# One scaled product per chunk instead of seven levels of pairwise decays, with the old way kept in a conditional block

## The chip, the cores and the metric

The kernel runs on one core of one Trainium2 chip. The metric is device time in microseconds from one launch. Before the change the median of three runs is 1061.55 us (1060.96 to 1065.03).

## The reference, cut to what matters

A linear recurrence with a decay per head and channel, and then a dense layer. B, H, S, D are 4, 8, 768, 48; there are 3072 tokens of width 384, and the dense layer is 2048 wide. The decays `w` are drawn between 0.85 and 0.95; the weights of the dense layer come as float64.

```
for t in range(S):
    cur = einsum('bhd,bhe->bhde', u[None] * kt, vt)
    y[:, :, t] = einsum('bhd,bhde->bhe', rt, state + cur)
    state = w[None, :, :, None] * state + einsum('bhd,bhe->bhde', kt, vt)
x = y.transpose(0, 2, 1, 3).reshape(B * S, H * D)
h = x @ w_in
out = (h - tanh(h)) @ w_out
```

## The kernel before

**First part.** Time is cut into 6 chunks of 128 steps. A unit (`unit`, L186) is one chunk of one batch, all 8 heads; there are 24 units, in order of chunk, then batch. Two heads share the 128 partitions (64 each, of which 48 are used), so a unit has four pairs of heads. Within a chunk, step t reads step s < t with the weight w^(t-1-s). The kernel never forms a negative power: it takes blocks of 128, 64, ... 2 steps, and pairs the steps of a block's first half with those of its second. For each of the six larger sizes POOL multiplies the turned r with powers (`rl`, L218), DVE the turned k (`kl`, L221); TensorE then makes the product of each of the seven levels (`lev`, L246, four pairs of heads, each product two instructions), and a copy puts it into the table `at`: ScalarE for the first level (L248), DVE under a mask for the other six (L250). `lev` has two buffers. Then `y_p` (L261, L265) applies `at` to v and, from the second chunk, the scaled r (`rs`, L232) to the state; `kv_p` (L273) makes the state's increment from `kn` (L228); three transposes (L289) lay the tokens out for the second part. The turned k and r come from transposes (L199) through one buffer and ScalarE copies (L201, L204). The step's own product through `u` is made on POOL (`rk`, L207 and L208) and DVE.

**Second part.** `dense` (L294) takes a block of two units' tokens; there are 12 blocks. For each of eight pairs of columns of `w_in` it makes `h` (L301), then on ScalarE, POOL and DVE h - tanh(h) with a series where h is small (L312 to L321), and two pairs later the product with `w_out` (L327). The output goes out by two DMAs per block (L343).

**Weights.** 28 pieces of float64 are loaded through two staging buffers by DMAs on ScalarE's queue (L147) and turned into float32 by one ScalarE, five DVE and two POOL instructions each (L154 to L161).

**Order.** `weave` (L357) interleaves the steps of several streams in proportion: the units of blocks 0 and 1 with the weights, then each dense block j with the units of block j + 2. Within that, a planner that works with estimated times sets the order of each engine's instructions. Every engine then runs its own list in order. At the start POOL clears thirty buffers (L119) that keep zeros, and DVE grows tables of powers by doubling (L88 to L94).

Of the kernel before, what the change touches and what calls it, by code (L numbers as in the profile page):

```python
# [25 lines left out]
@with_exitstack  # L26
def kernel(
    ctx: ExitStack,
    tc: tile.TileContext,
    r: bass.AP,  # L30
    k: bass.AP,
    v: bass.AP,
    w: bass.AP,
    u: bass.AP,
    moe_w_in: bass.AP,
    moe_w_out: bass.AP,
    out: bass.AP,
):
    nc = tc.nc
    V, A, T, G = nc.vector, nc.scalar, nc.tensor, nc.gpsimd  # L40

    B, H, S, D = r.shape
    DM, DFF = moe_w_in.shape
    C = 128                  # steps of time in a chunk
    PAD = 64                 # partitions of a head where two of them share the 128
    NP = H // 2              # pairs of heads
    NCH = S // C
    NU = NCH * B             # units of work: a chunk of one batch, all heads
    NK = DM // 128
    NF = DFF // 128  # L50
    L = 2                    # units in a block of the dense part
    NT = L * C
    SIZES = [128, 64, 32, 16, 8, 4, 2]
    AHEAD = 2
    HEAD = [slice(i * PAD, i * PAD + D) for i in range(2)]   # partitions of a pair's heads

    const = ctx.enter_context(tc.tile_pool(name="const", bufs=1))
    load = ctx.enter_context(tc.tile_pool(name="load", bufs=3))
    stage = ctx.enter_context(tc.tile_pool(name="stage", bufs=2))
    work = ctx.enter_context(tc.tile_pool(name="work", bufs=2))  # L60
    gpool = ctx.enter_context(tc.tile_pool(name="gpool", bufs=6))
    ps_a = ctx.enter_context(tc.tile_pool(name="ps_a", bufs=1, space=PSUM))
    ps_d = ctx.enter_context(tc.tile_pool(name="ps_d", bufs=2, space=PSUM))

    def fixed(name, shape, dt=F32):
        return const.tile(shape, dt, name=name, tag=name)

    ident = fixed("ident", [128, 128])
    make_identity(nc, ident)

# [4 lines left out]
    with nc.allow_non_contiguous_dma(reason="384 numbers, once"):  # L75
        for i in range(2):
            nc.sync.dma_start(out=wcol[i * PAD : i * PAD + D, :], in_=w.rearrange("(p i) d -> i d p", i=2)[i])
    ub = fixed("ub", [128, H, D])
    nc.sync.dma_start(
        out=ub.rearrange("p h d -> p (h d)"),  # L80
        in_=bass.AP(tensor=u.tensor, offset=u.offset, ap=[[0, 128], [1, H * D]]),
    )
# [50 lines left out]
    w_in_sb = fixed("w_in_sb", [128, NK, DFF])  # L133
    w_out_sb = fixed("w_out_sb", [128, NF, DM])
# [3 lines left out]
    def weight(dst, src, cols):  # L138
        if src.dtype == F32:
            return lambda: nc.scalar.dma_start(out=dst, in_=src)  # L140
        # Bits of float64 to float32, rounded to the nearest: the upper word gives sign, exponent
        # and 20 bits; the lower word, scaled to the exponent, is added.
# [23 lines left out]
    for q in range(DFF // 512):  # L166
        for ko in range(NK):
            sl = slice(q * 512, (q + 1) * 512)
            weights.append(weight(w_in_sb[:, ko, sl], w_in_v[:, ko, sl], 512))
        for f in range(4 * q, 4 * q + 4):  # L170
            weights.append(weight(w_out_sb[:, f, :], w_out_v[:, f, :], DM))

# [13 lines left out]
    def unit(n, xt, slot):  # L186
        """Steps of unit n; the last writes its tokens, transposed, to xt[:, :, slot, :]."""
        c, b = divmod(n, B)
        if n + AHEAD < NU:
            fetch(n + AHEAD)  # L190
# [4 lines left out]
        rT = rTs[n % 2]      # rT[:, p, i]: head 2 p + i, zero on the other head's partitions  # L195
# [9 lines left out]
        # The step's own key and value, through u.  # L205
# [86 lines left out]

# [1 line left out]
    def dense(j, xt):  # L294
        outs = [ps_d.tile([128, DM], F32, name=f"o{i}", tag=f"o{i}", bufs=1) for i in range(L)]

        def first(f):
            h = ps_d.tile([128, 2, NT], F32, name="h", tag="h")
            for z in range(2):
                for kk in range(NK):  # L300
                    T.matmul(h[:, z], w_in_sb[:, kk, (f + z) * 128 : (f + z + 1) * 128],  # L301
                             xt[:, kk].rearrange("p b t -> p (b t)"),
                             start=kk == 0, stop=kk == NK - 1)
            hf = h.rearrange("p z t -> p (z t)")

            def tmp(name):
                return work.tile([128, 2 * NT], F32, name=name, tag=name)

            s, th, q1, q2, cube, small = (tmp(x) for x in ("s", "th", "q1", "q2", "cube", "small"))
            g = gpool.tile([128, 2, NT], F32, name="g", tag="g")  # L310
            gf = g.rearrange("p z t -> p (z t)")
            A.activation(s, hf, AF.Square)  # L312
            A.activation(th, hf, AF.Tanh)  # L313
            A.activation(q1, s, AF.Square, bias=m1b)  # L314
            A.activation(q2, s, AF.Square, bias=m2b)  # L315
# [20 lines left out]
        for pair in waiting:  # L336
            second(*pair)
# [78 lines left out]
```

## Time and profile before

| | |
|---|---|
| runs, median (lowest to highest) | 1061.55 us (1060.96 to 1065.03) |
| profiled execution, span from first to last instruction | 1065.4 us; no time outside it is listed |
| instructions | 12106 |
| TensorE matmul, weight load | 80%, 63% of the span |
| DVE, POOL, ScalarE | 69%, 56%, 30% |
| DMA | 32.43 MB, 30 GB/s on the mean |

A busy share is an average over stages. Which stage is limited by what is read from tables over stretches of the span, and from who waited for whom. Matmuls are pipelined: one instruction lasts longer than the distance from its start to the next one's start, and the ends are modelled; the rate is read from starts.

### The profile page before, as it was taken

What the parts mean: (1) busy time and instruction counts of PE and PEld (TensorE: products, weight loads), DVE (VectorE), ACT (ScalarE), POOL (GpSimd) and SP (SyncE); (2) the same over time, 40 slices, a digit from 0 to 9 for tenths busy, and PEclk for the clock granted to TensorE, in tenths of its full rate; (3) what the DMA queues carried; (4) which work ended last, traced back from release to release, by engine and by line L of the source; (5) the groups of instructions that cost most, each with busy time, mean ns of one, the idle gap of its engine ahead of it and who ended that gap; (6) DMA issues with size and microseconds to landing.
All of it is one profiled execution on the core that took longest, in us unless ns stands there. A gap on an engine that the chain in (4) does not pass through costs nothing.

```text
span 1065.4 us, 12106 instructions
## 1 busy us (share of the span) xinstructions
PE 852.5 (80%) x4236; PEld 674.1 (63%) x4236; DVE 739.0 (69%) x1063; ACT 316.9 (30%) x558; POOL 595.9 (56%) x602
## 2 busy tenths in 40 slices
PE   0536676569898797798798797898888898899998
PEld 0426555447686686676676676676676676677775
DVE  7757898998765665675675575576576586775764
ACT  0111331231341341431431431431431431342443
POOL 8677866877762662653653653744743643561322
PEclk9956866798898998999998998989998999999999
DMA  6132232230110110110110110110110100000000
GB/s 114 42 94 62 62 95 48 78 82 1 38 24 1 37 23 1 38 23 1 38 23 1 38 23 1 38 23 1 38 23 1 38 8 1 16 0 16 1 15 15
DMA packets 82987, 32.43 MB, mean 30 GB/s; under 512 B 76144, under 2 KB 79344, under 8 KB 82928
## 3 DMA queue, kind: packets, MB, share of 16 engines
q1 hardware_dynamic: 78896, 19.08, 8.5%
q10 hardware_dynamic: 4032, 12.58, 3.8%
q8 instruction: 34, 0.56, 0.2%
q14 instruction: 25, 0.20, 0.1%
HBM read 26.94 MB, written 4.72 MB: 30 GB/s over the span
## 4 chain that ended last, share of the span: by engine, by line
PE 34%; POOL 30%; DVE 20%; issue 11%; ACT 3%; DMA 1%; POOLq 0%; DVEq 0%; ACTq 0%
POOL rl L218 20%; PE h L301 11%; PE o L327 10%; POOL small L316 5%; DVE at L250 4%; PE lev L246 4%; PE y_p L265 4%; DVE cube L319 3%; DVE cube L320 2%; POOL rk L207 2%; POOL rk L208 2%; DVE kl L221 2%; PE kv_p L273 2%; PE y_p L261 2%; DVE cube L317 1%
## 5 line engine op out<-in xcount | busy, mean ns | idle before, releaser
L316 POOL TENSOR_SCALAR small<-s 128x512 f32<-128x512 f32 x96 | 149.4, 1562 | 262.3 <-ACT s L312 251.6
L301 PE MATMUL h<-xt,w_in_sb 128*128 128x256 f32 x1152 | 292.2, 394 | 1.6 <-DVE g L318 1.5
L246 PE MATMUL lev<-rl,kl 128*128 128x128 f32 x1152 | 188.1, 322 | 129.1 <-DVE at L250 84.3
L218 POOL TENSOR_TENSOR rl<-rT,up 48x256 f32<-48x256 f32 x288 | 253.5, 892 | 52.0 <-ACT rT L204 31.0
L327 PE MATMUL o<-w_out_sb,g 128*128 128x384 f32 x768 | 272.2, 496 | 6.5 <-DVE g L321 6.5
L246 PEld LDWEIGHTS lev<-rl,kl 128*128 128x128 f32 x1152 | 173.4, 230 | 163.3 <-POOL rl L218 63.5
L301 PEld LDWEIGHTS h<-xt,w_in_sb 128*128 128x128 f32 x1152 | 216.0, 199 | 30.6 <-DVE g L318 2.5
L327 PEld LDWEIGHTS o<-w_out_sb,g 128*128 128x128 f32 x768 | 145.0, 194 | 86.0 <-DVE g L321 8.4
L312 ACT ACTIVATE s<-h 128x512 f32<-128x512 f32 x96 | 57.4, 598 | 385.0 <-PE h L301 154.3
L250 DVE COPY_PREDICATED at<-mask,lev 128x512 f32<-128x512 int32 x144 | 129.8, 901 | 17.9 <-PE lev L246 16.8
L321 DVE COPY_PREDICATED g<-small,cube 128x512 f32<-128x512 int32 x96 | 87.2, 908 | 53.7 <-POOL small L316 50.8
L221 DVE TENSOR_TENSOR kl<-kT,down 128x256 f32<-128x256 f32 x144 | 93.8, 694 | 37.7 <-ACT kT L201 37.7
L317 DVE SCALAR_TENSOR_TENSOR cube<-s,h 128x512 f32<-128x512 f32 x96 | 65.5, 682 | 59.4 <-ACT th L313 58.7
L320 DVE SCALAR_TENSOR_TENSOR cube<-q,cube 128x512 f32<-128x512 f32 x96 | 75.7, 788 | 7.1
L265 PE MATMUL y_p<-vt,at 128*128 128x48 f32 x384 | 60.0, 289 | 23.5 <-DVE at L250 23.0
L265 PEld LDWEIGHTS y_p<-vt,at 128*128 128x128 f32 x384 | 55.1, 212 | 31.3 <-DVE at L250 31.3
L319 DVE SCALAR_TENSOR_TENSOR cube<-q,cube 128x512 f32<-128x512 f32 x96 | 70.5, 734 | 0.0
L314 ACT ACTIVATE q<-s,m1b 128x512 f32<-128x512 f32 x96 | 69.4, 723 | 3.6 <-DVE cube L319 3.6
L315 ACT ACTIVATE q<-s,m2b 128x512 f32<-128x512 f32 x96 | 69.0, 719 | 1.2 <-DVE cube L320 1.0
L318 DVE TENSOR_TENSOR g<-h,th 128x512 f32<-128x512 f32 x96 | 65.6, 683 | 0.0
L313 ACT ACTIVATE th<-h 128x512 f32<-128x512 f32 x96 | 56.9, 593 | 0.0
L155 DVE TENSOR_SCALAR part<-st 128x384 uint32<-128x384 uint32 (+1 forms) x28 | 34.3, 1224 | 23.9 <-DMA st<-in_moe_w_out_dram 13.1
(69 smaller groups left out, 713.6 us busy)
## 6 DMA issues: line engine op xcount, KB each, us to landing
st<-in_moe_w_in_dram ACTq DMA_DIRECT2D x12, 512.0 KB, 4.1
st<-in_moe_w_out_dram ACTq DMA_DIRECT2D x16, 384.0 KB, 3.0
vt<-in_v_dram SPq DMA_DIRECT2D x24, 192.0 KB, 2.7
kt<-in_k_dram SPq DMA_DIRECT2D x24, 192.0 KB, 2.8
rt<-in_r_dram SPq DMA_DIRECT2D x24, 192.0 KB, 3.0
out_dram<-o SPq DMA_DIRECT2D x24, 192.0 KB, 1.9
ub<-in_u_dram SPq DMA_DIRECT2D x1, 192.0 KB, 5.8
wcol<-in_w_dram SPq DMA_DIRECT2D x2, 0.8 KB, 6.9
```

The source lines that it names most:

```text
L218: G.tensor_tensor(rls[n_][HEAD[i], :, i], rT[HEAD[i], :, i, :].rearrange(halves, b=nb)[:, :, :, m:], up[HEAD[i], :, None, 0:m].to_broadcas ...
L221: V.tensor_tensor(kls[n_].rearrange(halves, b=nb)[:, :, :, 0:m], kT.rearrange(halves, b=nb)[:, :, :, 0:m], down[:, :, None, C - m :].to_br ...
L246: T.matmul(lev[:, p].rearrange("s i b j -> s i (b j)"), lhsT, rhs, start=True, stop=True)
L250: V.copy_predicated(at.rearrange("s p i (b j) -> s (p i) b j", b=nb)[:, :, :, m:], masks[n_][:, None].to_broadcast([128, H, nb, m]), lev.r ...
L265: T.matmul(y_p[:, p, i, :], at[:, p, i, :], vt[:, 2 * p + i, :], start=c == 0, stop=True, skip_group_check=True)
L301: T.matmul(h[:, z], w_in_sb[:, kk, (f + z) * 128 : (f + z + 1) * 128], xt[:, kk].rearrange("p b t -> p (b t)"), start=kk == 0, stop=kk == ...
L316: G.tensor_scalar(small, s, SMALL, None, ALU.is_lt)
L317: V.scalar_tensor_tensor(cube, s, C4, hf, ALU.mult, ALU.mult)
L319: V.scalar_tensor_tensor(cube, q1, K1, cube, ALU.add, ALU.mult)
L320: V.scalar_tensor_tensor(cube, q2, K2, cube, ALU.add, ALU.mult)
L321: V.copy_predicated(gf, small.bitcast(I32), cube)
L327: T.matmul(outs[i], g[:, z, i * C : (i + 1) * C], w_out_sb[:, f + z, :], start=f + z == 0, stop=f + z == NF - 1)
```

## The change

The kernel body is split into functions. `near` is the new first part, for decays from 0.7 to 1.4. Within a chunk, w^(t-1-s) is w^t times w^-(s+1): r is scaled with w^t (`w_up`) and k with w^-(s+1) (`w_down`) before the transposes, and one product per head over all 128 steps replaces the seven levels. A mask keeps s < t. The scaled r serves the state's part as well, and the scaled k the state's increment, which is then multiplied by w^128. The tables come from a scan and a reciprocal; a decay outside the limits is replaced by 1 in them, and a flag is set to 1 if there is any such decay. At the end all engines read the flag, and `anywhere`, which is the old first part with a dense part of its own, is run under a condition. The dense part, the weights and the weaving are the same, but a unit counts as 6 steps there instead of 10.

```diff
+def near(ctx, tc, r, k, v, w, u, out, shared, weights):
...
+    def inside(name, x):
+        sq, ok = (fixed(f"{name}{i}", list(x.shape)) for i in range(2))
+        V.tensor_tensor(sq, x, x, ALU.mult)
+        V.tensor_scalar(ok, sq, W_LOW**2, None, ALU.is_ge)
+        V.tensor_scalar(sq, sq, W_HIGH**2, None, ALU.is_le)
+        V.tensor_tensor(ok, ok, sq, ALU.mult)
+        return ok
...
+    V.tensor_copy(by[:, :, 1:], wcol[:, :, None].to_broadcast([128, NP, C]))
...
+    V.tensor_tensor_scan(power.rearrange(flat), by.rearrange(flat), plus.rearrange(flat), 0.0, ALU.mult, ALU.add)
+    V.reciprocal(inverse, power)
...
+    w_up = turned("w_up", power, 0)
+    w_down = turned("w_down", inverse, 1)
...
+    V.tensor_reduce(okn, inside("okr", wrow), axis=mybir.AxisListType.X, op=ALU.min)
+    V.tensor_scalar(shared["flag"], okn, -1.0, 1.0, ALU.mult, ALU.add)
...
+    kws = zeroed("kw", 2, [128, H, PAD])
+    rws = zeroed("rw", 2, [128, H, PAD])
+    ats = [zeroed(f"at{i}_", 2, [128, NP, C]) for i in range(2)]
+    states = zeroed("state", B, [128, NP, 2, D])
...
+        for name, src in (("kt", k), ("rt", r), ("vt", v)):
+            t = load.tile([128, H, D], F32, name=name, tag=name)
+            nc.sync.dma_start(out=t, in_=src[b, :, rows, :].rearrange("h t d -> t h d"))
...
+    def unit(n, xt, slot):
...
+        G.tensor_tensor(kw[:, :, :D], kt, w_down, ALU.mult)
+        G.tensor_tensor(rw[:, :, :D], rt, w_up, ALU.mult)
+        turned = []
+        for name, src in (("kT", kw), ("rT", rw)):
+            ps = ps_a.tile([128, NP, C], F32, name="t_p", tag="tp")
+            for p in range(NP):
+                T.transpose(ps[:, p, :], src[:, 2 * p : 2 * p + 2, :].rearrange("t h d -> t (h d)"), ident)
+            t = work.tile([128, NP, C], F32, name=name, tag=name)
+            A.copy(t, ps)
...
+        lev = [ps_a.tile([128, NP, C], F32, name=f"lev{i}", tag=f"lev{i}") for i in range(2)]
+        for p in range(NP):
+            for i in range(2):
+                T.matmul(lev[i][:, p], kT[HEAD[i], p, :], rT[HEAD[i], p, :], start=True, stop=True)
+        yield
+        for i in range(2):
+            V.copy_predicated(at[i], before[:, None].to_broadcast([128, NP, C]), lev[i])
+        yield
...
+            both = state.rearrange("d p i e -> d p (i e)")
+            G.tensor_tensor(both, both, wn[:, :, None].to_broadcast([128, NP, 2 * D]), ALU.mult)
...
+    drive(d, work, unit, dense, fetch, weights, 6)
...
+    far = nc.values_load(flag[0:1, 0:1], min_val=0, max_val=1,
+                         skip_runtime_bounds_check_because="a comparison's 0 or 1")
+    with tc.If(far > 0):
+        anywhere(tc, r, k, v, w, u, out, shared)
```

## Rows read from the trace of the kernel before

**Rows 1.** Page: span and busy us (share of the span) xinstructions.
```profile
span 1065.4 us, 12106 instructions
PE 852.5 (80%) x4236; PEld 674.1 (63%) x4236; DVE 739.0 (69%) x1063; ACT 316.9 (30%) x558; POOL 595.9 (56%) x602
```

**Rows 2.** Page: chain that ended last, shares of the span by line.
```profile
POOL rl L218 20%; PE h L301 11%; PE o L327 10%; POOL small L316 5%; DVE at L250 4%; PE lev L246 4%; PE y_p L265 4%; DVE cube L319 3%; DVE cube L320 2%; POOL rk L207 2%; POOL rk L208 2%; DVE kl L221 2%; PE kv_p L273 2%; PE y_p L261 2%; DVE cube L317 1%
```

**Rows 3.** Timeline of SP, output DMAs: start us, duration us, what, count.
```profile
265.77 1.00 SPq L343 DMA_DIRECT2D out_dram<-o  x2
...
830.75 1.00 SPq L343 DMA_DIRECT2D out_dram<-o  x2
...
```

**Rows 4.** Windows: stretch, length, busy per engine, granted clock, DMA share, GB/s.
```profile
20.90:265.80 244.90, 154.81 (x719) 127.44 (x719) 202.15 (x303) 51.15 (x89) 180.66 (x172) 0.78 0.22 61
...
508.10:588.40 80.30, 68.04 (x360) 53.99 (x359) 52.45 (x76) 24.86 (x44) 42.66 (x42) 0.96 0.09 20
...
1020.20:1062.00 41.80, 41.75 (x161) 30.06 (x159) 26.44 (x40) 19.38 (x35) 12.29 (x8) 1.00 0.03 10
```

**Rows 5.** Timeline, 6 to 22 us.
```profile
6.96 14.24 DVE L155 TENSOR_SCALAR part<-st 128x512 uint32<-128x512 uint32 x1 [5.92 <-DMA st<-in_moe_w_in_dram]
...
19.43 1.49 POOL L119 MEMSET state<- 128x384 f32 x4
```

**Rows 6.** Waits of PE, 266 to 974 us: total us, times, longest.
```profile
PE lev L246 <- DVE at L250: 82.7, 43, 4.4
PE lev L246 <- POOL rl L218: 13.2, 9, 1.8
```

**Rows 7.** Timeline of PE, 597 to 628 us, a unit's instructions in full streams.
```profile
597.19 2.05 PE L246 MATMUL lev<-rl,kl 128*128 128x128 f32 x16 [1.41 <-POOL rl L218]
599.08 1.25 PE L301 MATMUL h<-xt,w_in_sb 128*128 128x256 f32 x5
...
621.52 0.43 PE L261 MATMUL y_p<-state,rs 128*128 128x96 f32 x2
...
622.19 0.43 PE L261 MATMUL y_p<-state,rs 128*128 128x96 f32 x2
...
624.89 1.03 PE L273 MATMUL kv_p<-vt,kn 128*128 128x96 f32 x8
625.75 0.49 PE L289 MATMUL x_p<-ident,y 128*128 128x128 f32 x3
```

**Rows 8.** Groups by line and form: count | busy us, mean ns | idle before.
```profile
L246 PE MATMUL lev<-rl,kl 128*128 128x128 f32 x1152 | 188.1, 322 | 129.1 <-DVE at L250 84.3 <-POOL rl L218 43.6
...
L155 DVE TENSOR_SCALAR part<-st 128x512 uint32<-128x512 uint32 x12 | 22.9, 1905 | 10.8 <-DMA st<-in_moe_w_in_dram 10.7
L228 POOL TENSOR_TENSOR kn<-kt,wkn 128x384 f32<-128x384 f32 x20 | 21.8, 1089 | 32.9 <-PE kv_p L273 32.8
```

**Rows 9.** Windows of one line each: L221 (`kl`), L250, L232 (`rs`), L218 (`rl`).
```profile
20.90:265.80 244.90, 30.95 (x36) 0.78 0.22 61
...
20.90:265.80 244.90, 32.55 (x36) 0.78 0.22 61
...
20.90:265.80 244.90, 4.39 (x4) 0.78 0.22 61
...
508.10:588.40 80.30, 21.11 (x24) 0.96 0.09 20
```

**Rows 10.** Timeline of POOL, the last instruction of a weight: two in a row, the last.
```profile
102.72 1.72 POOL L161 TENSOR_TENSOR w_in_sb<-w_in_sb,part 128x512 f32<-128x512 f32 x1
108.11 1.33 POOL L161 TENSOR_TENSOR w_in_sb<-w_in_sb,part 128x512 f32<-128x512 f32 x1
...
249.07 1.33 POOL L161 TENSOR_TENSOR w_out_sb<-w_out_sb,part 128x384 f32<-128x384 f32 x1
```

**Rows 11.** Page, DMA issues: count, KB each, median us to landing.
```profile
out_dram<-o SPq DMA_DIRECT2D x24, 192.0 KB, 1.9
...
wcol<-in_w_dram SPq DMA_DIRECT2D x2, 0.8 KB, 6.9
```

More of the change, by code (lines that the diff above doesn't have):

```diff
@@ L23, with weave @@
 M2, K2 = -2.2310246528459308, 2.3491904342222876
-@with_exitstack
[L27 to L38, printed above, removed]
+W_LOW, W_HIGH = 0.7, 1.4
+C = 128
+PAD = 64
+AHEAD = 2
+L = 2
+def weave(*streams):
+    done = [0] * len(streams)
+    live = [True] * len(streams)
+    while any(live):
+        i = min((i for i in range(len(streams)) if live[i]), key=lambda i: (done[i] + 1) / streams[i][1])
+        done[i] += 1
+        if next(streams[i][0], StopIteration) is StopIteration:
+            live[i] = False
@@ new lines, with __init__, load_decay @@
+class Dims:
+    def __init__(self, r, moe_w_in):
+        self.B, self.H, self.S, self.D = r.shape
+        self.DM, self.DFF = moe_w_in.shape
+        self.NP = self.H // 2
+        self.NCH = self.S // C
+        self.NU = self.NCH * self.B
+        self.NK = self.DM // 128
+        self.NF = self.DFF // 128
+        self.NT = L * C
+        self.NB = self.NU // L
+        self.HEAD = [slice(i * PAD, i * PAD + self.D) for i in range(2)]
+def load_decay(nc, wcol, w, d):
+    with nc.allow_non_contiguous_dma(reason="384 numbers, once"):
+        for i in range(2):
+            nc.sync.dma_start(out=wcol[d.HEAD[i], :], in_=w.rearrange("(p i) d -> i d p", i=2)[i])
@@ new lines, in drive, with block, each @@
+def drive(d, work, unit, dense, fetch, weights, nstep):
+    xts = {}
+    def block(j):
+        xts[j] = work.tile([128, d.NK, L, C], F32, name="xt", tag="xt", bufs=3)
+        for i in range(L):
+            yield from unit(L * j + i, xts[j], i)
+    def each(fs):
+        for f in fs:
+            f()
+            yield
+    for n in range(AHEAD):
+        fetch(n)
+    half = len(weights) // 2
+    for j, some in enumerate((weights[:half], weights[half:])):
+        weave((block(j), nstep * L), *([(each(some), len(some))] if some else []))
+    for j in range(d.NB):
+        streams = [(dense(j, xts.pop(j)), d.NF // 2 + 1)]
+        if j + 2 < d.NB:
+            streams.append((block(j + 2), nstep * L))
+        weave(*streams)
@@ L39 @@
+@with_exitstack
+def near(ctx, tc, r, k, v, w, u, out, shared, weights):
     nc = tc.nc
     V, A, T, G = nc.vector, nc.scalar, nc.tensor, nc.gpsimd
[L42 to L63, printed above, removed]
+    d = shared["dims"]
+    H, D, NP, NK, B, HEAD = d.H, d.D, d.NP, d.NK, d.B, d.HEAD
@@ new lines, in near @@
+    ok = inside("okc", wcol)
+    V.tensor_tensor(wcol, wcol, ok, ALU.mult)
+    V.tensor_scalar(ok, ok, -1.0, 1.0, ALU.mult, ALU.add)
+    V.tensor_tensor(wcol, wcol, ok, ALU.add)
+    by = fixed("by", [128, NP, C + 1])
+    plus = fixed("plus", [128, NP, C + 1])
+    power = fixed("power", [128, NP, C + 1])
+    inverse = fixed("inverse", [128, NP, C + 1])
+    V.memset(by[:, :, 0:1], 0.0)
+    V.tensor_copy(by[:, :, 1:], wcol[:, :, None].to_broadcast([128, NP, C]))
+    V.memset(plus, 0.0)
+    V.memset(plus[:, :, 0:1], 1.0)
@@ new lines, in zeroed @@
+    def zeroed(name, count, shape):
+        tiles = [fixed(f"{name}{i}", shape) for i in range(count)]
+        for t in tiles:
+            G.memset(t, 0.0)
+        return tiles
+    kws = zeroed("kw", 2, [128, H, PAD])
+    rws = zeroed("rw", 2, [128, H, PAD])
+    ats = [zeroed(f"at{i}_", 2, [128, NP, C]) for i in range(2)]
+    states = zeroed("state", B, [128, NP, 2, D])
+    dense = make_dense(nc, work, gpool, ps_d, shared["w_in"], shared["w_out"], shared["m1b"],
+                       shared["m2b"], out, d)
@@ L73 @@
     wcol = fixed("wcol", [128, NP])
     V.memset(wcol, 0.0)
-    with nc.allow_non_contiguous_dma(reason="384 numbers, once"):
-        for i in range(2):
-            nc.sync.dma_start(out=wcol[i * PAD : i * PAD + D, :], in_=w.rearrange("(p i) d -> i d p", i=2)[i])
+    load_decay(nc, wcol, w, d)
     ub = fixed("ub", [128, H, D])
[L79 to L82, printed above, removed]
+    load_bonus(nc, ub, u, d)
@@ L188, in unit @@
         c, b = divmod(n, B)
-        if n + AHEAD < NU:
+        if n + AHEAD < d.NU:
             fetch(n + AHEAD)
@@ L346 @@
-    m1b, m2b = fixed("m1b", [128, 1]), fixed("m2b", [128, 1])
-    V.memset(m1b, M1)
-    V.memset(m2b, M2)
-    def block(j):
-        xt = work.tile([128, NK, L, C], F32, name="xt", tag="xt", bufs=3)
-        xts[j] = xt
-        for i in range(L):
-            yield from unit(L * j + i, xt, i)
-    def weave(*streams):
-        done = [0] * len(streams)
-        live = [True] * len(streams)
-        while any(live):
-            i = min((i for i in range(len(streams)) if live[i]), key=lambda i: (done[i] + 1) / streams[i][1])
-            done[i] += 1
-            if next(streams[i][0], StopIteration) is StopIteration:
-                live[i] = False
@@ L367, in each @@
-    def each(fs):
-        for f in fs:
-            f()
-            yield
-    xts = {}
-    NSTEP = 10 * L
-    for n in range(AHEAD):
-        fetch(n)
-    half = len(weights) // 2
-    weave((block(0), NSTEP), (each(weights[:half]), half))
-    weave((block(1), NSTEP), (each(weights[half:]), len(weights) - half))
-    NB = NU // L
-    for j in range(NB):
-        streams = [(dense(j, xts.pop(j)), NF // 2 + 1)]
-        if j + 2 < NB:
-            streams.append((block(j + 2), NSTEP))
-        weave(*streams)
+    dense = make_dense(nc, work, gpool, ps_d, shared["w_in"], shared["w_out"], shared["m1b"],
+                       shared["m2b"], out, d)
@@ new lines, in anywhere, with kernel, fixed @@
+    drive(d, work, unit, dense, fetch, [], 10)
+@with_exitstack
+def kernel(
+    ctx: ExitStack,
+    tc: tile.TileContext,
+    r: bass.AP,
+    k: bass.AP,
+    v: bass.AP,
+    w: bass.AP,
+    u: bass.AP,
+    moe_w_in: bass.AP,
+    moe_w_out: bass.AP,
+    out: bass.AP,
+):
+    nc = tc.nc
+    d = Dims(r, moe_w_in)
+    const = ctx.enter_context(tc.tile_pool(name="const", bufs=1))
+    def fixed(name, shape, dt=F32):
+        return const.tile(shape, dt, name=name, tag=name)
+    ident = fixed("ident", [128, 128])
+    make_identity(nc, ident)
+    m1b, m2b = fixed("m1b", [128, 1]), fixed("m2b", [128, 1])
+    nc.vector.memset(m1b, M1)
+    nc.vector.memset(m2b, M2)
+    w_in_sb = fixed("w_in_sb", [128, d.NK, d.DFF])
+    w_out_sb = fixed("w_out_sb", [128, d.NF, d.DM])
+    flag = fixed("flag", [1, 1], I32)
+    shared = {"dims": d, "ident": ident, "m1b": m1b, "m2b": m2b, "w_in": w_in_sb, "w_out": w_out_sb,
+              "flag": flag}
+    with tc.tile_pool(name="stage", bufs=2) as stage:
+        weights = weight_steps(nc, stage, w_in_sb, w_out_sb, moe_w_in, moe_w_out, d)
+        near(tc, r, k, v, w, u, out, shared, weights)
+    far = nc.values_load(flag[0:1, 0:1], min_val=0, max_val=1,
+                         skip_runtime_bounds_check_because="a comparison's 0 or 1")
+    with tc.If(far > 0):
+        anywhere(tc, r, k, v, w, u, out, shared)
```

269 lines of the change are left out of this document (188 added, 81 removed).

## The prediction

> **What bounds the kernel now.** I read the page from the top: the span, then the busy shares. [rows 1] TensorE is busy 80% of 1065.4 us and no other engine reaches 70%. The chain that ended last [rows 2] spreads over PE, POOL and DVE, and its longest single line is POOL's `rl` products, 20%: so TensorE is the engine with most to do, but it is often late because its inputs are. That average hides three stages, so I cut the span at the issues of the output DMAs, one pair per dense block [rows 3]: the first pair leaves at 265.8, the eighth at 830.8 (seven equal periods, 80.7 us each), then two shorter periods, and the last blocks need 41.8 each. The table over these stretches [rows 4] shows what each is limited by:
>
> - 0 to 20.9: DVE sits in one instruction. It begins at 6.96, takes 14.24 us and ends when POOL's row of memsets ends at 20.9 [rows 5].
> - 20.9 to 265.8: DVE is busy 202 of 245 us (82.5%), TensorE 63%. Here weights are converted, on DVE and POOL, among six units.
> - an interior block: TensorE 68.0 of 80.3. A block without units: 41.75 of 41.8, so the dense chain alone keeps TensorE full; it is two units that make it 80.7.
>
> TensorE's waits inside the interior stretch [rows 6] have one cause: 82.7 us of `lev` products waiting for the DVE copies of an earlier level, 13.2 on POOL's `rl`. 708 us hold 8.8 blocks, so this is 10.9 us per block.
>
> **The change, part by part.**
>
> *TensorE in a unit.* Instructions in a full stream, from start to the next start [rows 7]: 16 `lev` in 1.89 us (0.118 each), one pair of heads in `y_p` 0.67 (so 2.7 per unit), eight `kv_p` 0.86, or 0.108 each; at that pace the eight transposes ahead take 0.86 and the three behind 0.33. A unit now has 7 levels x 4 pairs x 2 passes = 56 `lev` instructions, 6.6 us; with the rest (0.86 + 2.7 + 0.86 + 0.33) 11.3 us. After it has 4 pairs x 2 heads x 2 passes = 16, 1.9 us, and the rest stays: 6.6 us. The new products use 48 rows instead of 128, a form that this trace doesn't have. Upper bound: each exposed for the 322 ns that one `lev` lasts [rows 8], 5.2 us a unit; lower: the two heads, on separate rows, overlap wholly, 0.95. I take 1.9, the rate of the nearest row.
>
> [...]
>
> *Waits in an interior block.* [...] The waits come from a chain of seven levels through two `lev` buffers, each emptied by a DVE copy that stands in line with dense work. After, a unit has one such step: 16 products, two copies (0.90 us each, 36 in 32.6 [rows 9]), then `y_p`. What is late next: the copies stand behind up to one set of dense DVE work, and the transposes now wait for POOL's two new products, `kw` and `rw` (1.09 each by `kn`, the same shape [rows 8]); the ScalarE copies between the transposes stay, one per tile. POOL falls from 42.7 us per block to about 24 (less 21.1 for `rl` [rows 9], less two `kn`, plus four of 1.09), DVE's 52.5 loses at least eight of twelve copies, 7 us, so both have room, and dense products are there to fill TensorE. [...] I take 3, nearer to zero since the wait named by rows 6 goes and a pure dense block shows none. An interior block is then 41.8 + 13.2 + 3 = 58.0. Nine follow the first; the last two carry units without `kv_p` (four units, 0.86 each): 9 x 58.0 - 3.4 = 518.6.
>
> *Start to the first output.* DVE is the fullest engine, so I count its work. Of its 202.2 us in that stretch go `kl` 31.0, the level copies 32.6 and `rs` 4.4 [rows 9]; 12 copies come back, 10.9. The new tables have a scan and a reciprocal over 516 columns and a dozen small ones, in place of the old doubling; neither operation is in the trace. Bounds: 0.9 us each (a copy of 512 columns [rows 9]) and 1.9 (the longest mean of a 512-column DVE group, L155 [rows 8]); both are little, so I let the new tables cost what the old ones did. That leaves 145 us. At the same busy share, 0.825, it takes 176. The start moves up as well: POOL clears twelve buffers instead of thirty, some 6 us (four of 384 columns take 1.49 [rows 5], eight more have 512), so DVE is free at 8 instead of 21. First output at 8 + 176 = 184 instead of 265.8. Bounds: DVE without a gap, 8 + 145 = 153; or the conversion keeps its pace. That pace is 8.2 us per weight (28 of them between 20.9 and 250.4, while two in a row can be 5.4 apart [rows 10]); at 8.2 the last of them would end 13 earlier, by the earlier start alone, and the first output leave near 253.
>
> *DMA queues.* SP issues the same three loads per unit, now into dense tiles, and one 1.5 KB row of decays more; nothing on it waits for zeroed tiles any more. A load is issued two units ahead, so this is nothing either way. ACT's queue, which issues the weights, keeps its two staging buffers; its wait for a buffer holds ScalarE's copies of the unit, as now.
>
> *The conditional block.* All engines read a flag and jump over a second copy of the old kernel. This stands behind all other work, so nothing hides it and nothing waits but the end. The trace has no jump. Bounds: 1.9 us, the shortest median of a DMA to landing, and 13.8, twice the longest small one, 6.9 [rows 11] (one trip for the flag, one for instructions). Below nothing is excluded, as it is only added. I take 5.
>
> [...]
>
> *Sum.* 184 + 518.6 + 83.6 (the last two blocks) + 3.4 (end of the last block at 1062.0 to the span's end) + 5 = 795, against the span of 1065.4: a quarter less. The span is that execution's own time, as nothing around it is listed. The median of the runs is 0.4% under it, so 792.
>
> **Rivals.**
>
> 1. *The waits stay* (0.12). The order is planned with estimates; if the single `lev` buffer per head and POOL's `kw` cost TensorE as much per block as now, it is 9 x 13.3 = 120 more: 912. For it: POOL's and DVE's queues are in order. Against: two copies instead of seven stand in the way.
> 2. *The start doesn't shrink* (0.13): staging, not DVE, sets the pace. First output at 253: 861. For it: no engine is full while weights come (DVE 82.5%, POOL 181 of 245 us [rows 4]); against it, the weights that come 5.4 us apart.
> 3. *Better than that* (0.14): heads overlap (1.9 less per block, 17) and no waits (27): 748.
> 4. *The block runs* (0.01): slower. The flag is 1 as soon as one of 384 decays lies outside 0.7 to 1.4. Then the old kernel follows whole, some 1060 more: 1850. The inputs draw decays from 0.85 to 0.95, and both ends of that lie inside.
>
> **From these to the numbers.** The forecast holds 0.60, alone from 765 to 830. The range, 738 to 868, takes in rivals 2 and 3 and the upper bound of the new products (3.3 us more a unit, 59 in nine blocks, 850); outside it are rivals 1 and 4. A measurement of this kernel tells about 0.5% from no change: faster by more than that 0.98, within it 0.01, slower 0.01.
>
> **What would show it.** In the profile after: the output pairs 57 to 60 us apart; the first at 175 to 195; the `lev` stream at 0.12 us an instruction; TensorE's longest wait on the copies of `at` or on POOL's `kw`, about 3 us a block; DVE's first conversion not held by memsets; a few us without work at the end. It is wrong if the period stays above 65, if the first output leaves after 230, or if the last one is followed by tens of us.

## The result, and the profile after

The changed kernel takes 768.87 us (median of four runs, 767.96 to 770.07), against 1061.33 in the same session: ratio 0.722, 95% interval 0.7189 to 0.7251. The forecast was 792, its range 738 to 868.

The page of the changed kernel, against [rows 1] (the profiled run took 770.07 us):

```profile
span 768.3 us, 9268 instructions
PE 678.2 (88%) x3280; PEld 513.8 (67%) x3280; DVE 532.9 (69%) x779; ACT 289.7 (38%) x511; POOL 379.9 (49%) x312
```

Its chain by line, against [rows 2]:

```profile
PE h L129 31%; PE o L155 28%; PE y_p L354 5%; PE lev L342 3%; PE y_p L350 3%; PE t_p L323 2%; POOL part L103 2%; PE kv_p L362 2%; DVE cube L148 2%; DMA st<-in_moe_w_in_dram 2%; DVE cube L147 1%; DVE part L98 1%; DVE st L100 1%; DVE g L149 1%; POOL rk L330 1%
```

The chain is now mostly the dense products; POOL's 20% for `rl` is gone. SP's output DMAs, against [rows 3]: first, second, eighth and ninth pair.

```profile
200.63 1.00 SPq L171 DMA_DIRECT2D out_dram<-o  x2
247.91 1.00 SPq L171 DMA_DIRECT2D out_dram<-o  x2
...
574.74 1.00 SPq L171 DMA_DIRECT2D out_dram<-o  x2
626.51 0.98 SPq L171 DMA_DIRECT2D out_dram<-o  x2
```

Below, the *first output* is the start of the first pair, and the *period* the distance from one pair to the next in the interior. Five of the six gaps between the second and the eighth pair are 54.66 us, where they were 80.7. The saving of 297 us in the span is 65 to the first output (265.8 to 200.6), 191 over the next seven (565.0 to 374.1) and 44 over the two after them; the last two blocks take 83.6 as before, and the end is 2.9 longer. Windows, as in [rows 4]: the first instructions, the rest of the start, one interior block, the last block.

```profile
0.00:7.50 7.50, 0.00 (x0) 0.00 (x0) 6.03 (x11) 2.61 (x3) 6.25 (x20) 1.00 0.77 208
7.50:200.60 193.10, 122.28 (x541) 92.02 (x542) 171.83 (x241) 47.43 (x85) 146.37 (x118) 0.85 0.36 91
...
411.90:466.60 54.70, 53.80 (x280) 41.28 (x279) 34.72 (x52) 22.65 (x40) 24.59 (x20) 1.00 0.13 30
720.00:761.90 41.90, 41.85 (x161) 30.04 (x159) 26.40 (x40) 19.49 (x35) 12.29 (x8) 1.00 0.03 11
```

The interior block is TensorE's: 53.8 of 54.7 at the full granted clock (0.96 of it before). In the start DVE is the fullest engine: 171.8 of 193.1, or 89%. All that TensorE waited for from 248 to 626 us, against [rows 6], and a unit's products in its timeline, against [rows 7]:

```profile
PE o L155 <- DVE g L149: 4.5, 5, 0.9
```

```profile
412.28 1.03 PE L129 MATMUL h<-xt,w_in_sb 128*128 128x256 f32 x4
413.14 0.63 PE L323 MATMUL t_p<-ident,rw 128*128 128x128 f32 x4
413.61 1.89 PE L129 MATMUL h<-xt,w_in_sb 128*128 128x256 f32 x8
415.43 1.16 PE L342 MATMUL lev<-rT,kT 48*128 48x128 f32 x16
416.52 5.45 PE L129 MATMUL h<-xt,w_in_sb 128*128 128x256 f32 x24
```

From start to next start the 16 `lev` instructions take 1.09 us. A unit on TensorE is then 5.8 us (4.75 for the rest, as forecast), a block 41.75 + 2 x 5.8 = 53.4, and only 1.3 of the 54.66 are left for waits and gaps. The interior's 26.0 us per block are thus about 11.0 of TensorE's own work (two units, each 6.6 less 1.09) and 15.0 of time in which it waited or ran more slowly. The clock has a part in the latter: between 567.2 and 574.0 us of the kernel before, at a granted clock of 0.50, eight `lev` take 1.84 us from their start to that of the next instruction, and right behind, at 1.00, they take 0.89. No run changes the clock alone.

### The profile page after: what moved, and what is told of

The parts are those of the page before. It is cut to its first block, busy times and chain, and to the rows that moved or that the text cites. A ratio compares the mean times of both kernels' runs of the same rounds, so it can differ in the third digit from the quotient of the medians.

```text
span 768.3 us, 9268 instructions
## 1 busy us (share of the span) xinstructions
PE 678.2 (88%) x3280; PEld 513.8 (67%) x3280; DVE 532.9 (69%) x779; ACT 289.7 (38%) x511; POOL 379.9 (49%) x312
## 4 chain that ended last, share of the span: by engine, by line
PE 74%; DVE 12%; POOL 7%; issue 3%; DMA 2%; ACT 1%; ACTq 0%; DVEq 0%; POOLq 0%
PE h L129 31%; PE o L155 28%; PE y_p L354 5%; PE lev L342 3%; PE y_p L350 3%; PE t_p L323 2%; POOL part L103 2%; PE kv_p L362 2%; DVE cube L148 2%; DMA st<-in_moe_w_in_dram 2%; DVE cube L147 1%; DVE part L98 1%; DVE st L100 1%; DVE g L149 1%; POOL rk L330 1%
## 5 line engine op out<-in xcount | busy, mean ns | idle before, releaser
L129 PE MATMUL h<-xt,w_in_sb 128*128 128x256 f32 x1152 | 280.2, 390 | 11.9 <-POOL w_in_sb L104 11.6
L155 PEld LDWEIGHTS o<-w_out_sb,g 128*128 128x128 f32 x768 | 147.9, 195 | 108.7 <-DVE g L149 12.9
L149 DVE COPY_PREDICATED g<-small,cube 128x512 f32<-128x512 int32 x96 | 85.6, 892 | 5.2
L148 DVE SCALAR_TENSOR_TENSOR cube<-q,cube 128x512 f32<-128x512 f32 x96 | 80.0, 834 | 8.2
L147 DVE SCALAR_TENSOR_TENSOR cube<-q,cube 128x512 f32<-128x512 f32 x96 | 74.8, 779 | 0.0
L354 PE MATMUL y_p<-vt,at 128*128 128x48 f32 x384 | 58.9, 282 | 12.9 <-DVE at L345 12.9
L354 PEld LDWEIGHTS y_p<-vt,at 128*128 128x128 f32 x384 | 55.5, 208 | 17.7 <-DVE at L345 15.3
L336 POOL TENSOR_TENSOR dv<-vt,du 128x384 f32<-128x384 f32 x24 | 24.2, 1007 | 60.5 <-DVE y L357 60.5
L103 POOL TENSOR_TENSOR part<-part,st 128x384 f32<-128x384 f32 (+1 forms) x28 | 35.8, 1279 | 26.0 <-issue 14.1
L318 POOL TENSOR_TENSOR rw<-rt,w_up 128x384 f32<-128x384 f32 x24 | 29.2, 1217 | 38.2 <-PE t_p L323 37.4
L377 ACT COPY xt<-x_p 128x384 f32<-128x384 f32 x24 | 11.5, 480 | 83.7 <-PE x_p L376 83.7
L342 PEld LDWEIGHTS lev<-rT,kT 48*128 48x128 f32 x384 | 27.3, 212 | 23.1 <-ACT rT L325 13.8
L342 PE MATMUL lev<-rT,kT 48*128 48x128 f32 x384 | 32.5, 313 | 11.3 <-ACT rT L325 11.3
```

The lines of the kernel that those rows point to most:

```text
L147: V.scalar_tensor_tensor(cube, q1, K1, cube, ALU.add, ALU.mult)
L148: V.scalar_tensor_tensor(cube, q2, K2, cube, ALU.add, ALU.mult)
L149: V.copy_predicated(gf, small.bitcast(I32), cube)
L155: T.matmul(outs[i], g[:, z, i * C : (i + 1) * C], w_out_sb[:, f + z, :], start=f + z == 0, stop=f + z == d.NF - 1)
L342: T.matmul(lev[i][:, p], kT[HEAD[i], p, :], rT[HEAD[i], p, :], start=True, stop=True)
L354: T.matmul(y_p[:, p, i, :], at[i][:, p, :], vt[:, 2 * p + i, :], start=c == 0, stop=True, skip_group_check=True)
```

## Experiments on the kernel before: what held TensorE up

The planner orders every edited kernel anew, so an edit can also move other instructions in the queues. No run parts this from the edit itself; in b4 TensorE's list of an interior block is nearly that of the kernel before.

**b1_no_copies: the chain of copies alone.**

```diff
-                V.copy_predicated(at..., masks[n_]..., lev...)     # six smaller levels
```

> The kernel before with the six masked copies of a unit left out (the first level's ScalarE copy stays); all products are still made. Theory: in an interior block TensorE's 10.9 us of waits hang on these copies, which stand in line on DVE between dense work. Without them the lev waits are near 0, the period falls from 80.7 to about 70, and the clock comes nearer to full: total about 950 (nine blocks by some 10, the start by some 15 to 25). Rival (the waits are POOL's, through rl): the wait only changes its name to rl, the period stays above 77, total above 1010.

Measured: 942.9 us (941.24 to 944.56), ratio 0.8848 (0.8758 to 0.8939); first output 245.0, period 67.9. The times came as the theory had them. The waits on the copies are gone, but not all waits: those on `rl` were 5.7 us in this stretch before (300 to 600 us) and are now 18.0.

```profile
PE lev L246 <- POOL rl L218: 18.0, 15, 1.4
```

**b2_no_scaled: the copies stay, `rl` and `kl` go.**

```diff
-            for i in range(2):
-                G.tensor_tensor(rls[n_]..., ALU.mult)
-            V.tensor_tensor(kls[n_]..., ALU.mult)
```

> The kernel before with the scaled copies rl and kl left out (12 POOL and 6 DVE products a unit; the tables keep the zeros of the start); the seven levels' products and their copies stay. Theory (the copies set the waits in interior blocks): the period falls only by what POOL held back, 1 to 4 us, to 77 to 80; the start, where DVE is the fullest engine, loses 31 us of DVE work and its lev products no longer wait for rl (30 us there): first output near 225; total about 1000. Rival (POOL's rl, 20 per cent of the chain that ended last, sets the period): period 70 or less, total below 930.

Measured: 888.84 us (888.09 to 889.6), ratio 0.8341 (0.8262 to 0.8421); first output 211.3, period 66.4 (332 us over five blocks). My theory missed; the rival fits. All copies are there, and yet the wait on them nearly goes: 7.2 us in 300 to 600, where the kernel before has 35.0 (the edit takes seven lines out, so L239 is the old L246):

```profile
PE lev L239 <- DVE at L243: 7.2, 4, 2.1
PE y_p L258 <- DVE at L243: 0.5, 3, 0.2
```

So the copies were late because of something that went with `rl` or `kl`. This run takes POOL's `rl` and DVE's `kl` away together and does not part them.

**b3_no_levels: `rl` and `kl` stay, their products and copies go.**

```diff
-        for n_ in SIZES:
+        for n_ in SIZES[:1]:                                        # products and copies only
```

> The kernel before with the lev products of the six smaller levels and their masked copies left out; the first level and all rl and kl products stay, though most are not read. TensorE loses 48 of 56 lev instructions a unit, 5.7 us at the full rate, and the waits on the copies. Theory: the interior period becomes what TensorE has left, 41.8 + 2 x (11.3 - 5.7) = 53, plus 1 to 3 us of waits on rl: 54 to 56, as in the changed kernel (54.7), though POOL and DVE still make the scaled copies; total about 800. Rival (POOL's products and its queue matter by themselves): period 60 or more, total above 860.

Measured: 903.25 us (902.23 to 904.27), ratio 0.8476 (0.8394 to 0.8558); first output 259.4, period 64.9. The theory missed again, the rival fits: POOL's queue holds TensorE without any of the smaller levels in between. Timeline, with the wait in brackets:

```profile
506.22 8.29 POOL L218 TENSOR_TENSOR rl<-rT,up 48x256 f32<-48x256 f32 x9 [8.19 <-ACT rT L204]
...
514.48 1.48 POOL L316 TENSOR_SCALAR small<-s 128x512 f32<-128x512 f32 x1
516.05 1.97 POOL L218 TENSOR_TENSOR rl<-rT,up 48x256 f32<-48x256 f32 x3
...
520.13 1.49 POOL L316 TENSOR_SCALAR small<-s 128x512 f32<-128x512 f32 x1
```

The dense part's `small` stands behind nine `rl` products in a row. DVE's `g` (L321) needs it, TensorE's `o` needs `g`: `PE o L327 <- DVE g L321` is 36.1 us in 300 to 600, the longest 6.2. The same chain is in the kernel before (600 to 612 us), where it ends at `lev`:

```profile
599.90 6.23 POOL L218 TENSOR_TENSOR rl<-rT,up 48x256 f32<-48x256 f32 x7
...
608.24 2.94 POOL L316 TENSOR_SCALAR small<-s 128x512 f32<-128x512 f32 x2
609.76 1.12 DVE L321 COPY_PREDICATED g<-small,cube 128x512 f32<-128x512 int32 x1 [5.52 <-POOL small L316]
610.79 0.67 DVE L250 COPY_PREDICATED at<-mask,lev 128x512 f32<-128x512 int32 x1
...
611.61 2.05 PE L246 MATMUL lev<-rl,kl 128*128 128x128 f32 x8 [3.39 <-DVE at L250]
```

Read it downwards: POOL makes seven `rl` and two `rk` first and is late with `small`, so DVE stands 5.52 us before `g`; the copy queued behind `g` runs as soon as DVE is free; and TensorE's 3.39 us are put down to that copy, which is only the last link. From 266 to 974 us DVE's `g` waits for `small` in this way 11 times, 50.8 us in all.

**b4_small_on_dve: cut that link alone.**

```diff
-            G.tensor_scalar(small, s, SMALL, None, ALU.is_lt)
+            V.tensor_scalar(small, s, SMALL, None, ALU.is_lt)
```

> The kernel before with one instruction per dense step moved: the comparison that gives small goes from POOL to DVE; all work of the recurrence stays. Theory, formed after leaving out the copies took the period to 67.9 and leaving out the scaled copies to 66: the wait on the DVE copies begins on POOL. There the comparison stands behind up to twelve rl products, DVE's last dense instruction (g) waits for it, and the copies of the levels stand behind g. With small on DVE the chain is cut, though DVE gets 3 to 5 us a block more: period 69 to 73, total 970 to 1000. Rival (the copies themselves and the two lev buffers make the waits): period 78 or more, total above 1040, since DVE only gets more work.

Measured: 1002.51 us (1001.82 to 1003.2), ratio 0.9385 (0.9342 to 0.9427); first output 261.7, period 73.5. The period and the total are a little above the theory (69 to 73 and 970 to 1000). Moving one instruction of 1.5 us per dense step from POOL to the busier DVE gains 6% and removes 7 us of stall per block, with nothing of the recurrence changed. So this link is nearly half of the 16.3 us of stall in a block (80.7 less 41.8 of dense work and 22.6 of two units); what makes the other half stays open. The waits that are left (300 to 600 us) name copies and POOL:

```profile
PE lev L246 <- DVE at L250: 21.4, 12, 2.7
PE lev L246 <- POOL rl L218: 5.6, 4, 1.4
```

The three removals gain 12.8, 14.3 and 15.8 us per block one by one, together 43, where the whole change gains 26. Of b3's 15.8 us, 11.3 are TensorE's own work, and it still stands 11.8 above its remaining 53.1; so it frees only 4.5 of the 16.3 us of stall, where b1 and b2 free 12.8 and 14.3. The edits cut links of one chain, and b1 and b2 free mostly the same stall, so the gains may not be added.

## Experiments on the kernel after

Totals in this section stand against the 768.87 us of the changed kernel, through ratios to the same kernel before, each with an interval of 3 to 7 us on either side. Those of a1, a6 and a7 overlap the changed kernel's; what is said of these three rests on the traces.

**a1_by_head: order of the new products.**

```diff
-        for p in range(NP):
-            for i in range(2):
+        for i in range(2):
+            for p in range(NP):
                 T.matmul(lev[i][:, p], kT[HEAD[i], p, :], rT[HEAD[i], p, :], ...)
```

> The changed kernel with the sixteen lev instructions of a unit ordered by head (all four pairs of head 0, then of head 1) instead of alternating between the heads' rows. Theory: the alternating ones run at 0.068 us each (16 in 1.09 us) because neighbours sit on different rows and overlap; in a row on the same rows they run at 0.107 to 0.118, so 16 take 1.7 to 1.9 us, the interior period rises by 1.3 to 1.6 us to 56, the total by 10 to 18 us to about 783. Rival (48 rows are simply faster to load): still 1.1 us, total 769 within 3.

Measured: 777.8 us (777.22 to 778.38), ratio 0.7299 (0.723 to 0.7368); period 55.76. Timeline of TensorE:

```profile
417.30 1.71 PE L342 MATMUL lev<-rT,kT 48*128 48x128 f32 x16
418.94 1.35 PE L129 MATMUL h<-xt,w_in_sb 128*128 128x256 f32 x5
```

The same 16 instructions take 1.64 us instead of 1.09. Only the order differs. Two heads lie on separate rows, and that alternating ones overlap is the reading that fits; 1.09 is near the forecast's lower bound (0.95, for whole overlap). The difference of two units, 1.1, is the whole difference of the period.

**a2_lev4: the products four times over.**

```diff
+        for again in range(4):
             for p in range(NP):
```

> The changed kernel with each lev product made four times over (64 instead of 16 instructions a unit; the last one counts). Theory (TensorE is the only bound of an interior block): 48 more at 0.068 us are 3.3 us a unit, 6.5 us a block: period 61.2, total 769 + 9 x 6.5 + some in the start = 830 to 845, TensorE still without waits. Rival (there is slack, or another engine sets the period): period below 58, total below 800.

Measured: 835.79 us (835.56 to 836.01), ratio 0.7837 (0.7811 to 0.7864); first output 210.8, period 60.02. 64 instructions take 3.77 us:

```profile
454.41 3.84 PE L343 MATMUL lev<-rT,kT 48*128 48x128 f32 x64
458.18 1.99 PE L129 MATMUL h<-xt,w_in_sb 128*128 128x256 f32 x8
```

48 more cost 2.68, or 0.056 each; the first 16 are then 0.90 and some 0.2 that comes once per stretch. The period grows by 5.36 = 2 x 2.68, all of it: the interior has no slack on TensorE.

**a3_copies3: the two copies three times over.**

```diff
+        for again in range(3):
             for i in range(2):
                 V.copy_predicated(at[i], ...)
```

> The changed kernel with its two masked copies a unit made three times, so that there are six as before: DVE gets 2.9 us a unit more, and y_p waits for the last of them. Theory: in an interior block DVE has room (35 of 54.7 us), so the period rises by 0 to 2 us; in the start, where DVE is busy 89 per cent, seven units cost 7 x 2.9 = 20 us: first output near 218, total 785 to 805. Rival (the DVE time of the copies itself made the old waits): the period rises by 5 us or more, total above 830.

Measured: 785.2 us (784.67 to 785.73), ratio 0.7363 (0.7336 to 0.739). The total is as expected, its place is not: the first output stays (200.1), the second is 9 us later (256.9), the period is 55.5. DVE is no busier before the first output than without the extra copies (169.2 us from 7.5 to 200.1), so other work was put behind it. In the interior the eight more copies of 0.73 us each, 5.8 per block, cost 0.9: the dense products hide them.

**a4_chain: four rounds through one buffer, as the old levels had.**

```diff
-        lev = [ps_a.tile([128, NP, C], ...) for i in range(2)]
...
+        for p in range(NP):
+            lev = [ps_a.tile([128, C], F32, name=f"lev{i}", tag=f"lev{i}") for i in range(2)]
+            for i in range(2):
+                T.matmul(lev[i], kT[HEAD[i], p, :], rT[HEAD[i], p, :], start=True, stop=True)
+            for i in range(2):
+                V.copy_predicated(at[i][:, p, :], before, lev[i])
```

> The changed kernel with the lev product made in four rounds of one pair of heads each, all through one buffer per head, each round followed by its two small masked copies: the same TensorE instructions and the same columns copied, but a chain through buffers as before. Theory (the old waits were the chain, one wait of about 1 us per round): with 8 rounds a block the waits of lev on the copies return, 4 to 8 us a block: period 59 to 63, total 810 to 850. Rival (the amount of work made them, not the chain): period within 1.5 us of 54.7, total 769 to 785.

Measured: 822.04 us (821.08 to 823.0), ratio 0.7709 (0.7675 to 0.7742); first output 210.6, period 59.5. The size was expected, the cause was not: nothing waits on the copies (TensorE's one wait is again `o` on `g`, 5.7 us in 378). The time is TensorE's own. Its timeline:

```profile
444.31 0.49 PE L342 MATMUL lev<-rT,kT 48*128 48x128 f32 x4
444.73 0.70 PE L129 MATMUL h<-xt,w_in_sb 128*128 128x256 f32 x2
445.36 0.51 PE L342 MATMUL lev<-rT,kT 48*128 48x128 f32 x4
445.81 2.43 PE L129 MATMUL h<-xt,w_in_sb 128*128 128x256 f32 x10
448.16 0.49 PE L342 MATMUL lev<-rT,kT 48*128 48x128 f32 x2
448.58 0.70 PE L129 MATMUL h<-xt,w_in_sb 128*128 128x256 f32 x2
```

By starts, four `lev` take 0.42 to 0.45 (0.22 at 0.056 each), two `h` behind them 0.63 (0.44 at the 0.22 each that 24 in a row show). So about 0.2 us are lost at each change between 48-row and 128-row products, in both directions. Between products of 128 rows no such loss shows: in the changed kernel's timeline above, four `h` between transposes take 0.86 us and the four transposes behind them 0.47. Pieces of two `lev` belong to one head and take 0.42 as well, as fits one head's products without overlap: two at the 0.1025 of a1 make 0.21, four at 0.056 make 0.22. The planner fills the gaps of the chain with other products, so the gaps become changes: a block has twelve pieces of `lev` instead of two. Twenty more changes make 4.0 of the 4.8 us, and the overlap that eight pieces of two lack some 0.7 (at the 0.1025 of a1).

**a5_no_guard: two of DVE's five instructions per weight left out.**

```diff
-            V.tensor_scalar(hi, hi, 20, 0x7FF, ALU.logical_shift_right, ALU.bitwise_and)
-            V.scalar_tensor_tensor(dst, hi, 897.0, dst, ALU.is_ge, ALU.mult)
```

> The changed kernel without the two DVE instructions per weight that clear numbers too small for float32 (none of the weights here is): DVE loses 45 of its 172 us in the start. Theory (DVE sets the pace of the start): the first output comes 35 to 45 us earlier, near 160, and the total falls to about 730. Rival (the two staging buffers and their loads set the pace, 6.6 us a weight): the first output moves by less than 12 us, total above 757.

Measured: 751.66 us (749.53 to 753.78), ratio 0.7049 (0.6996 to 0.7101). The first output leaves at 172.9 (27.7 earlier), the second at 227.5 (20.4 earlier), the period stays 54.67. The gain lies between the theory (35 to 45 us earlier) and the rival (less than 12). DVE is busy for 131.7 us from 7.5 to 172.9, 40 less than in the changed kernel, and POOL, with 140.9, is now the fuller engine: DVE's work holds the start back, but not alone.

**a6_no_block: without the flag and the second copy of the old kernel.**

```diff
-    far = nc.values_load(flag[0:1, 0:1], min_val=0, max_val=1, ...)
-    with tc.If(far > 0):
-        anywhere(tc, r, k, v, w, u, out, shared)
```

> The changed kernel without the flag's reading and the conditional block at its end. Theory: the block costs what lies behind the last output: 6.3 us from the last ScalarE copy to the end of the span against 3.4 before, so the total falls by 2 to 4 us, to about 766; nothing else moves. Rival (it also holds something earlier, or costs nothing): a fall of over 8 us, or under 1.

Measured: 765.9 us (765.38 to 767.52), ratio 0.7172 (0.7145 to 0.7198). The intervals overlap, so the total alone doesn't show the 3 us; the ends do. With the block the last copy begins at 762.0 and the span ends at 768.3; without it 761.2 and 764.7: 6.3 against 3.5 us.

**a7_stage4: four staging buffers instead of two.**

```diff
-    with tc.tile_pool(name="stage", bufs=2) as stage:
+    with tc.tile_pool(name="stage", bufs=4) as stage:
```

> The changed kernel with four staging buffers for the weights instead of two. Theory (DVE and POOL set the pace of the start, as the run without the two DVE instructions moved the first output by 28 of 45 us): the first output comes 0 to 12 us earlier, total 757 to 769. Rival (two buffers set the pace): first output before 175, total below 745.

Measured: 775.63 us (773.96 to 777.3), ratio 0.7261 (0.7224 to 0.7298). POOL's last weight sum ends at 153.9 instead of 194.4, and yet the first output doesn't move (200.6) and the second is 7.3 later (255.2). The start in this kernel, and what TensorE waits for in it (0 to 205 us):

```profile
0.00:200.60 200.60, 107.49 (x491) 85.12 (x492) 179.01 (x243) 47.05 (x82) 147.00 (x136) 0.82 0.37 95
```

```profile
PE y_p L354 <- DVE at L345: 44.9, 8, 15.8
```

DVE is as busy as in the changed kernel, 179.0 us against 177.9 to the same time. Weights that come earlier only push the units back: the wait of `y_p` on the copies is 44.9 us, in the changed kernel 12.9. So staging is not the pace. The theory had no loss in it: it gave a total of 757 to 769.

**a8_trunc: POOL's part of a weight left out.**

```diff
-            A.activation(lo_f, lo, AF.Copy, scale=2.0**-52)
...
+            V.scalar_tensor_tensor(bits, lo, 29, bits, ALU.logical_shift_right, ALU.bitwise_or)
...
-            V.tensor_scalar(part, bits, 0xFF800000, None, ALU.bitwise_and)
-            G.tensor_tensor(part_f, part_f, lo_f, ALU.mult)
-            G.tensor_tensor(dst, dst, part_f, ALU.add)
```

> The changed kernel with the weights converted on DVE alone: one DVE instruction shifts the top three bits of the lower word in and ORs them, in place of ScalarE's lower-word copy, DVE's exponent mask and POOL's two products and sums. The last bit of a weight is cut off instead of rounded. Theory: the start is paced by DVE's busy time, and that is long because POOL works beside it (the five DVE instructions of a weight take 113 us in all in the changed kernel, 65 to 72 at the shortest durations of the same forms, and POOL's two take 73). Without POOL's part DVE's instructions get shorter: DVE busy until the first output falls from 172 us to about 140, the first output leaves at 165 to 175 instead of 200.6, the period stays at 54.7, the total is 735 to 745. Rival: the DVE instructions last as long without POOL's part, so DVE's count of instructions decides, which is the same: first output within 8 us of 200.6, total 760 to 772.

Measured: 735.1 us (733.02 to 736.11), ratio 0.6888 (0.6841 to 0.6935): faster than both kernels. First output 164.1, second 213.8, period 54.66. As theory had it. Its start:

```profile
7.50:166.00 158.50, 113.81 (x552) 86.28 (x553) 137.42 (x242) 37.32 (x66) 73.55 (x58) 0.92 0.44 112
```

As many DVE instructions (242 against 241) take 137.4 us instead of 171.8, with POOL's work halved (146.4 to 73.6). Which of them got shorter is in the groups by form: of the changed kernel, to 200 us (count | busy us, mean ns),

```profile
L99 DVE SCALAR_TENSOR_TENSOR w_out_sb<-st,part 128x384 uint32<-128x384 uint32 x16 | 15.7, 982 | 0.2
...
L147 DVE SCALAR_TENSOR_TENSOR cube<-q,cube 128x512 f32<-128x512 f32 x9 | 10.7, 1188 | 0.0
L149 DVE COPY_PREDICATED g<-small,cube 128x512 f32<-128x512 int32 x9 | 10.4, 1155 | 0.1
...
L345 DVE COPY_PREDICATED at<-before,lev 128x512 f32<-128x512 int32 x14 | 10.1, 726 | 1.0 <-PE lev L342 1.0
...
L146 DVE TENSOR_TENSOR g<-h,th 128x512 f32<-128x512 f32 x9 | 6.1, 679 | 0.0
```

and of this one, to 170 us (its line numbers are one to three lower):

```profile
L98 DVE SCALAR_TENSOR_TENSOR w_out_sb<-st,part 128x384 uint32<-128x384 uint32 x16 | 11.7, 734 | 0.1
L342 DVE COPY_PREDICATED at<-before,lev 128x512 f32<-128x512 int32 x14 | 10.0, 724 | 0.0
...
L144 DVE SCALAR_TENSOR_TENSOR cube<-q,cube 128x512 f32<-128x512 f32 x10 | 7.8, 785 | 0.0
...
L143 DVE TENSOR_TENSOR g<-h,th 128x512 f32<-128x512 f32 x10 | 6.8, 681 | 0.0
L146 DVE COPY_PREDICATED g<-small,cube 128x512 f32<-128x512 int32 x9 | 6.5, 727 | 0.0
```

Instructions that take an operand from TensorE's result buffers (`lev`, `h`) are the same in both, 726 and 724, 679 and 681 ns. Those with both operands in the ordinary on-chip memory (SBUF) fall: 982 to 734, 1188 to 785, 1155 to 727, and by 21 to 37% over all seven such groups (the least is the other `cube` with `q`, 1063 to 839). But `tensor_scalar`, with a single operand in SBUF, falls as well, by 6 to 33% over four groups (712 to 670, 704 to 470), so two operands are not the whole distinction. (ScalarE's part of a weight, 17 us in all, went as well; the runs don't part it from POOL's.)

Shorter DVE instructions are not all of the gain. From 7.5 us to the second output, a5 and this run make the same 769 TensorE instructions, and DVE is busy for 166.9 and 167.7 us; yet a5 takes 220.1 us and this run 206.3, with POOL busy for 166.3 and 100.0. So POOL's part of a weight, or ScalarE's, costs time besides what it adds to DVE's. No run takes that part away and leaves DVE's durations as they were.

## Why the prediction was right, and where its sizes were off

*The stages and the bound: right.* TensorE's own work per block was forecast as 55.0 (41.8 + 13.2) and is 53.4; a2's added products appear in the period whole. Term by term, from the sum of 794.6 to the span of 768.3: the start is 16.6 longer, the nine blocks between first output and tail take 477.8 instead of 518.6 (−40.8), the tail is as forecast, the end 2.1 shorter. The start was late and the blocks early, beyond the signs that were named for either (first output 175 to 195, period 57 to 60); that the two errors partly cancel in the total is luck.

*"16 `lev` in 1.9 us": mis-sized, 1.09.* The rate came from 128-row products. The 48-row ones take 1.09 when heads alternate and 1.64 by head (a1); the overlap that fits this was rival 3's condition. This is 1.6 per block.

*"I take 3" for waits: mis-sized, 1.3.* Together with `lev` this makes the 3.3 from 58.0 to 54.66; the last two such blocks come to 103.7 instead of 112.6. But the cause that was given, a chain of levels each emptied by a copy, was only the last link. b2 removes nearly all of the wait without touching one copy, and b4 nearly half of the stall (7.2 of 16.3 us per block) by moving `small`. [rows 6] name the last link; where the chain can be followed, it begins at POOL's row of `rl`, which [rows 2] had at the top with 20%, `small` in fourth place. The change takes away the row of `rl` and most copies, so a small number came out although its cause was incomplete; that is luck too. Without the row of `rl`, even a chain of four rounds through one buffer doesn't wait (a4), which speaks against rival 1 (the waits stay); its 13.3 us a block are the 16.3 of stall before, less the 3. What TensorE does wait for, `o` on `g` (4.5 us in 378), is neither of the two waits that were named, on the copies or on `kw`.

*"That leaves 145 us" of DVE work at the start: mis-sized, 172.* I carried over DVE's time less what goes, and the busy share 0.825 (it became 0.89). By groups, the weights' five instructions on DVE take 113 us in all, about 101 before (without the one that was held), and the dense ones 43 for nine sets, 35 for eight before. Part of the difference is thus that more dense work and a seventh unit fall into the stretch, which goes with a first block of 47.3 and not 58: start and first block together are 247.9 against 242 forecast. The larger lesson is that durations in the start are not fixed: with POOL's and ScalarE's weight part beside them those of the two-operand forms were 27 to 59% longer than in a8. That staging is not the pace (rival 2), a7 shows; DVE's work is the larger part of it (a5, a8), and POOL's or ScalarE's part of a weight comes on top. The new tables, called little, cost 3.4 for the reciprocal, beyond my bound of 1.9, and 1.2 for the scan.

*"DVE's first conversion not held by memsets": right, but another instruction is.* DVE's timeline of the changed kernel:

```profile
2.68 4.40 DVE L237 TENSOR_SCALAR okr<-okr 1x384 f32<-1x384 f32 x1
7.12 0.35 DVE L238 TENSOR_SCALAR okr<-okr 1x384 f32<-1x384 f32 x1
...
7.47 0.41 DVE L98 TENSOR_SCALAR part<-st 128x512 uint32<-128x512 uint32 x1
```

The conversion begins at 7.47 and takes 0.41 us ([rows 5]: 14.24). The hold went to the decay check, 4.40 against 0.35 for the same form after it; it ends when POOL's clearing does (7.08 and 6.88 us), as before.

*"I take 5" for the conditional block: mis-sized, about 3* (a6). The flag's loads take 463 to 545 ns on each engine, and all but ScalarE's and SP's are done before the last copy at 762.0. The trip for instructions in the upper bound was my estimate: seven transfers of instructions fall between 760.0 us and the end, in the kernel before none in the last 8.4 us, but whether the end waits for them, no run shows.

## What to carry to other kernels

When a wait names an engine, look one link further: what did the named instruction itself stand behind in its queue, and who released that. Links of one chain may not be priced one by one and added, for cutting one can free most of the stall (b1 and b2: 12.8 and 14.3 of 16.3 us). Small products on part of the rows were cheapest here in one stretch, alternating between row groups: sixteen took 1.09 us, by head 1.64, and each further change of rows some 0.2 (a1, a4). And an engine's work, counted at its durations, is not a fixed sum: DVE's on two SBUF operands were 21 to 37% shorter with POOL's and ScalarE's part of a weight left out (a8).

## What the runs showed of the hardware

- Two heads' products on separate rows, in alternation, take 0.056 us an instruction in long streams and 0.068 in sixteens with the change included, by head 0.1025 (a1, a2): the reading that fits is overlap.
- A change between 48-row and 128-row products costs about 0.2 us each way, and no wait shows it (a4); between 128-row products of different kinds no such cost shows (four `h` 0.86, the four transposes behind them 0.47).
- With POOL's and ScalarE's part of a weight left out, DVE instructions whose operands both lie in SBUF are 21 to 37% shorter, `tensor_scalar` from SBUF 6 to 33%, and those that read TensorE's results as long as before (a8).
- A reciprocal over 516 columns takes 3.4 us, a scan over as many 1.2.
